# The first chunks of a fused linear-attention and SoLU kernel, written out by hand, with constant matrix products in TensorE's gaps

## The chip, the cores and the metric

The kernel runs on one core of one Trainium2 chip. The time is the device time of one execution in microseconds; the figure compared is the median of several executions. TensorE multiplies matrices out of SBUF into PSUM, VectorE, ScalarE and GpSimd work element by element, and SyncE here only issues DMAs. Each engine takes its instructions in the order in which they were written down, and waits by semaphore for what other engines or DMAs must deliver first.

## What is computed

Two layers follow each other. The first is linear attention with a decay (4 batches, 8 heads, 768 steps, 48 channels a head), the second a feed-forward layer whose activation is SoLU followed by a layer norm:

```python
for t in range(S):
    cur = np.einsum('bhd,bhe->bhde', u[None] * kt, vt)
    y[:, :, t] = np.einsum('bhd,bhde->bhe', rt, state + cur)
    state = w[None, :, :, None] * state + np.einsum('bhd,bhe->bhde', kt, vt)
x = y.transpose(0, 2, 1, 3).reshape(B * S, H * D)        # 3072 x 384
h = x @ w_in                                             # 384 x 1024
solu = h * softmax(h)
out = (layernorm(solu) * g_ln) @ w_out                   # 1024 x 384
```

r, k, v, w and u are float32; w_in, w_out and g_ln are handed over as given by numpy, the weights in float64.

## The kernel before

The sequence is cut into chunks of 128 steps, so there are 24 units (a batch and a chunk each), and `units` lists the first chunk of all four batches, then the second, and so on. Here "chunk 0, 1, 2 ..." means the unit with that index. For each unit:

- `load` fetches r, k and v (192 KB each) into rotating buffers (5 for r and k, 6 for v).
- `decay_k` (L672 to L676, GpSimd) multiplies k by the table `kdec`; `turn_r` and `turn_k` (TensorE) transpose r and k, four 128x128 transposes each; VectorE multiplies the transposed r by the table `fore` (L711), ScalarE copies the transposed k (L720). Chunk 0 takes its undecayed k instead, and VectorE multiplies by `back` (L722).
- `weigh` (two multiplications) and `sum_own` (a row sum on VectorE, L692) give the weight that u adds for a step's own key; `diagonal` writes it as eight 128x128 diagonals (ScalarE, L698) into the tile `AT`.
- `scores` multiplies k by r (TensorE, L733, 16 products, all chunks into the same PSUM tile `at`), then VectorE copies the upper triangle into `AT` with a mask (L735).
- `finish` multiplies v by `AT`, and the state by r from the second chunk of a batch on (TensorE, L760: "heads"), ScalarE copies the result to `xT` (L772), TensorE makes the state's increment (L778), and VectorE and GpSimd update the state (L784 to L787).
- `ffn_in` makes h, the input product: 128 x 384 times 384 x 1024, in two halves of 512 columns (L795), into one PSUM tile `h`, of which there is one buffer; ScalarE takes its exponential (L798).
- `unit` makes the activation and its sums (VectorE L805, L807; ScalarE L809, L810), `halve_ln` and `join_ln` transpose it by DMA, `ffn_out` makes the output product (L877) and stores it.

The weights come in 14 pieces (six of w_in, eight of w_out), as pairs of 32-bit words, and are turned into float32 on the chip: `load_weights` fetches a piece into one of six buffers, `convert_a` makes the low words (ScalarE, L517), `convert_b` the high words (VectorE, L530 and L532), `convert_c` adds them (GpSimd, L540). For the first six pieces `convert_b` uses the PSUM tile `h` as scratch. Pieces 0 to 2 are the three row blocks of w_in's first half of columns, 3 to 5 those of the second.

At the very start w is fetched (L482), transposed (L598) and turned on VectorE into powers and two tables (L599 to L609), whose transposes are `kdec` and `rdec` (L620, L621).

The order of all engines is written out by hand: under `manual_schedule` the instructions stand in each queue in the order of the program text. A loop from i = -2 interleaves the stages of different units; the feed-forward half of a unit lags `LA` = 2 and the output product another `LO` = 5 steps behind. Its first four steps, with a dictionary that says how many pieces each takes up, are the start:

```python
conversions = {-2: 1, -1: 1, 0: 2, 1: 2, 2: 2, 3: 2, 4: 2, 5: 2}
for i in range(-2, N + LA + LO):
    j, l = i - LA, i - LA - LO
```

PSUM tiles of the transposes, heads, state products and output products share the tag `m`, four buffers taken in turn; a buffer's next user waits until its last reader is through.

Of the kernel before, what the change touches and what calls it, by code (L numbers as in the profile page):

```python
# [399 lines left out]
def direct_path(  # L400
# [78 lines left out]
    wrow = const.tile([1, dm], F32, name="wrow")  # L479

    nc.vector.memset(wq, 1.0)
    nc.sync.dma_start(out=wq[:, :, 0:D], in_=w.rearrange("(a q) d -> a q d", q=2))  # L482
    nc.scalar.dma_start(out=u_bc.rearrange("p h d -> p (h d)"),
                        in_=u.rearrange("h d -> (h d)").partition_broadcast(128))
    for i in range(NLD):
# [34 lines left out]
    def convert_b(j):  # L520
        hi, low = step[j]
        n = low.shape[1]
        ma = wpool.tile([128, n], U32, tag="ma", name="ma", bufs=4)
        part = ma
        if pieces[j][2] is None:
            part = psH.tile([128, dff], F32, tag="h", name="part").bitcast(U32)[:, 0:n]

        nc.vector.tensor_scalar(out=part, in0=hi, scalar1=3, scalar2=0x3FFFFFF8,  # L530
                                op0=ALU.logical_shift_left, op1=ALU.bitwise_and)
        nc.vector.scalar_tensor_tensor(out=ma, in0=hi, scalar=0xC0000000, in1=part,  # L532
                                       op0=ALU.bitwise_and, op1=ALU.bitwise_or)
        step[j] = ma, low

    def convert_c(j):
        dst, _, f = pieces[j]
        ma, low = step[j]

        nc.gpsimd.tensor_tensor(out=dst.bitcast(U32) if f is None else ma, in0=ma, in1=low,  # L540
                                op=ALU.add)
# [21 lines left out]
    load(0, "kr")  # L563
    load_weights(0)
    load(1, "kr")
    load_weights(1)
    load(2, "kr")
    load_weights(2)
    load_weights(3)
    load(0, "v")  # L570
    load(3, "kr")
    load_weights(4)
    load(1, "v")
    load_weights(5)
    load(4, "kr")
    load(2, "v")

    ident = const.tile([128, 128], F32, name="ident")
    make_identity(nc, ident)
    for vt in vts:  # L580
        nc.gpsimd.memset(vt[:, :, D:], 0.0)
    neg_half = const.tile([128, 1], F32, name="neg_half")
# [4 lines left out]
    for St in states:  # L587
# [8 lines left out]
    nc.vector.memset(back[:, :, T - 1 : T], 1.0)  # L596
    wd_ps = psM.tile([128, HP], F32, tag="m", name="wd_ps")
    nc.tensor.transpose(wd_ps, wq.rearrange("a q d -> a (q d)"), ident[0:HP, 0:HP])  # L598
    nc.vector.tensor_scalar(out=pw[:, 0, 0], in0=wd_ps, scalar1=LOW, scalar2=HIGH,  # L599
                            op0=ALU.max, op1=ALU.min)  # L600
    for j in range(8):
# [123 lines left out]

    def scores(i):
        X = live[i]
        A4 = X["AT"].rearrange("p (a q) t -> p q a t", q=2)
        for a in range(HP):
            for c in range(2):  # L730
                for q in range(2):
                    rows = slice(q * P, q * P + D)
                    nc.tensor.matmul(pss[ts(c, P), q, a, c * P :], X["kT"][rows, a, ts(c, P)],  # L733
                                     X["rT"][rows, a, c * P :], start=True, stop=True)
        nc.vector.copy_predicated(A4, later.unsqueeze(1).to_broadcast([128, 2, HP, T]), pss)  # L735


# [8 lines left out]
    inner = [[(m,) + p for m in range(g, 12, 4) for p in parts(m)] for g in range(4)]  # L746
    inner = [group[n] for n in range(4) for group in inner]

    def finish(i):
        b, c = units[i]  # L750
        X = live[i]
        vt, AT, St = vts[i % NV], X["AT"], states[b]
        vf = vt.rearrange("p h d -> p (h d)")
        y_ps = psM.tile([128, KD, 128], F32, tag="m", name="y_ps")
        last = {m: n for n, (m, h, at) in enumerate(inner)}
        opened = set()

        def into(m, lhsT, rhs, stop):
            j, g = divmod(m, 4)
            nc.tensor.matmul(y_ps[32 * g : 32 * g + 32, j, :], lhsT, rhs, start=(g not in opened),  # L760
                             stop=stop, skip_group_check=True)
            opened.add(g)

        if c > 0:
            for m in range(12):
                a, n = divmod(m, 3)
                into(m, St[:, a].rearrange("p q d -> p (q d)")[:, ts(n, 32)], X["rT"][:, a, :],
                     False)
        for n, (m, h, at) in enumerate(inner):
            into(m, vf[:, at : at + 32], AT[:, h, :], last[m] == n)  # L770
        X["xT"] = fpool.tile([128, KD, 128], F32, name="xT", bufs=LA + 1)
        nc.scalar.copy(out=X["xT"], in_=y_ps)  # L772
        if c < C - 1:
            kv_ps = psM.tile([128, HP, D], F32, tag="m", name="kv_ps")
            for a in range(HP):
                for g in range(4):
                    h = 2 * a + g // 2
                    nc.tensor.matmul(kv_ps[ts(g, 32), a], X["kp"][:, h, ts(g % 2, 32)],  # L778
                                     vt[:, h, 0:D], start=True, stop=True)
            for q in range(2):  # L780
                wT = pw[ts(q, P), 0, 7].unsqueeze(2).to_broadcast([P, HP, D])
                S = St[ts(q, P), :, q]
                if c > 0:
                    nc.vector.tensor_add(S, kv_ps[ts(q, P)], S)  # L784
                    nc.gpsimd.tensor_mul(S, S, wT)  # L785
                else:
                    nc.vector.tensor_mul(S, kv_ps[ts(q, P)], wT)  # L787


    def ffn_in(i):  # L790
        X = live[i]
        h_ps = psH.tile([128, dff], F32, tag="h", name="h_ps")
        for n in range(dff // NX):
            for j in range(KD):
                nc.tensor.matmul(h_ps[:, ts(n, NX)], X["xT"][:, j, :], w_in_sb[:, j, ts(n, NX)],  # L795
                                 start=(j == 0), stop=(j == KD - 1))
        e = X["e"] = fpool.tile([128, dff], F32, name="e")
        nc.scalar.activation(out=e, in_=h_ps, func=ACT.Exp, accum_out=sums[:, i : i + 1])  # L798
        X["h"] = h_ps

    def unit(i):
        X = live[i]
# [78 lines left out]


    ahead = 6
    todo = list(range(len(pieces)))
    conversions = {-2: 1, -1: 1, 0: 2, 1: 2, 2: 2, 3: 2, 4: 2, 5: 2}
    now = []
    for i in range(-2, N + LA + LO):
        j, l = i - LA, i - LA - LO
        early = l < 0
        if i == -1:  # L890
            nc.sync.dma_start(out=g_sb, in_=moe_g_ln.rearrange("(c p) -> p c", p=128))
        if 0 <= i and i + 5 < N:
            load(i + 5, "kr")
        if 0 <= i and i + 3 < N:
            load(i + 3, "v")
        early_h = l <= 0
        if early_h and i >= LA:
            ffn_in(j)
        before, now = now, [todo.pop(0) for _ in range(conversions.get(i, 0))]
        for p in before:  # L900
            if pieces[p][2] is not None:
                convert_c(p)
        if i == -2:
            turn_r(0)
            turn_k(0)
            turn_table(back, kdec)
            weigh(0, nc.vector)
            decay_k(0)
            sum_own(0)
        for p in now:  # L910
            convert_a(p)
            if ahead < len(pieces):
                load_weights(ahead)
                ahead += 1
        if -2 < i and i + 2 < N:
            if i + 2 < FIRST:
                turn_r(i + 2)
            elif not early_h:
                join_rk(i + 2)
            if early_h and i >= LA:  # L920
                unit(j)
            if early_h and i + 2 >= FIRST:
                join_rk(i + 2)
            if i < 0 or i >= LA:
                sum_own(i + 2)
            if i + 2 < FIRST:
                turn_k(i + 2)
        if i < LA:
            for p in now:
                convert_b(p)  # L930
        if i == 0:
            sum_own(2)
        if i + 3 < N and i != 1:
            decay_k(i + 3)
            if i + 3 >= FIRST:
                decay_r(i + 3)
            if i < 0:
                weigh(i + 3, nc.gpsimd)
        for p in now if i < LA else []:
            convert_c(p)  # L940
        if i == 1:
            weigh(3, nc.gpsimd)
            decay_k(4)
        if 1 <= i and i + 3 < N:
            weigh(i + 3, nc.gpsimd)
        if 0 <= j - 1 < N:
            deviation(j - 1)
# [12 lines left out]
        if not early:  # L960
# [6 lines left out]
            if l == N - 1:  # L967
                check_sums()
            ffn_out(l)
        if 0 <= i + 1 < N:  # L970
            scores(i + 1)
        if i < 0:
            diagonal(i + 2)
        if 0 <= i < N:
            finish(i)
        if i == 1:
            turn_table(fore, rdec)
            sum_own(3)
        if early and 0 <= i:
            diagonal(i + 2)  # L980
        if i == 1:
            nc.vector.tensor_single_scalar(out=minus_g, in_=g_sb, scalar=-1.0, op=ALU.mult)
        if i >= LA:
            for p in before:
                convert_d(p)
            for p in now:
                convert_b(p)
    return bad


# [40 lines left out]
```

## Time and profile before

| | |
|---|---|
| median of 3 runs | 354.89 us (354.72 to 355.54) |
| the profiled execution | 355.35 us, of which the span of the program is 353.5 |
| TensorE busy | 338.0 us, 96% of the span |
| VectorE, ScalarE, GpSimd busy | 210.8, 242.1, 176.5 us |
| first instruction of TensorE | at 3.59 us |
| first input product starts | at 27.63 us |
| second input product starts | at 36.77 us |
| loads up to the sixth weight piece | landed at 24.04 us |

In lines of the profile, PE is TensorE, DVE is VectorE, ACT is ScalarE, POOL is GpSimd, SP is SyncE, and L733 is line 733 of the kernel. In lists by time the first column is the start in us after the span's begin and the second the length of that group; instructions of one kind that follow each other are merged, with their number behind an x (a float32 product is two instructions there, and a transpose one), and the square brackets tell how long the engine was idle before and what ended that. In the chain that ended last each line is a stretch of the one chain of dependent work, traced back from the end. In the list of waits the three figures are the sum in us, the number of times, and the longest.

### The profile page before, as it was taken

How to read it: one execution, taken by the hardware profiler on the slowest of the kernel's cores; microseconds unless marked ns; L12 is line 12 of the kernel's file. 1: busy time of each engine (PE TensorE's matmuls, PEld its weight loads, DVE VectorE, ACT ScalarE, POOL GpSimd, SP SyncE). 2: the span in 40 equal slices, each digit the busy share in tenths (PEclk: the TensorE clock that was granted, in tenths of full speed). 3: DMA queues.
4: the chain of work that ended last, by engine and by line, in shares of the span. 5: the costliest groups of instructions: out<-in, count | busy, mean ns of one | idle time of the engine just before them, and what ended most of it. 6: DMA issues, size and time to landing. Idle time of an engine off the chain costs nothing.

```text
span 353.5 us, 8407 instructions
## 1 busy us (share of the span) xinstructions
PE 338.0 (96%) x3427; PEld 204.8 (58%) x3427; DVE 210.8 (60%) x323; ACT 242.1 (68%) x457; POOL 176.5 (50%) x196
## 2 busy tenths in 40 slices
PE   2699999999999999999999999999999999999993
PEld 2485566656566556566566566565565565555563
DVE  7795888886468567665865765765771441323220
ACT  3765988988897667677867778778687464465510
POOL 3879667784865754945945846746730000000000
PEclk9999999999999999999999999999999999999998
DMA  7998997259999868988997979857663523551641
GB/s 164 266 237 183 252 209 126 51 105 162 189 186 163 150 122 154 195 174 185 188 159 174 206 146 184 187 130 146 150 129 62 126 69 59 128 126 47 139 105 33
DMA packets 164878, 52.75 MB, mean 149 GB/s; under 512 B 157917, under 2 KB 161246, under 8 KB 164830
## 3 DMA queue, kind: packets, MB, share of 16 engines
q1 hardware_dynamic: 164686, 51.92, 71.9%
q8 instruction: 29, 0.48, 0.6%
q10 hardware_dynamic: 144, 0.20, 0.2%
q14 instruction: 19, 0.16, 0.2%
HBM read 26.94 MB, written 4.72 MB: 90 GB/s over the span
## 4 chain that ended last, share of the span: by engine, by line
PE 90%; issue 3%; POOL 2%; DVE 2%; ACT 1%; DMA 1%; POOLq 0%; DVEq 0%
PE o_ps L877 35%; PE h_ps L795 35%; PE y_ps L760 10%; PE at L733 6%; PE kv_ps L778 2%; PE tk_ps L718 1%; PE tr_ps L710 1%; POOL kp L674 1%; DMA wq<-in_w_dram 1%; ACT AT L698 1%; POOL rku L687 1%; DVE part L530 0%; DVE ma L532 0%; POOL w_in_sb L540 0%; DVE solu L807 0%
## 5 line engine op out<-in xcount | busy, mean ns | idle before, releaser
L795 PE MATMUL h_ps<-w_in_sb,xT 128*128 128x512 f32 x288 | 129.8, 600 | 0.7 <-DVE solu L807 0.5
L877 PE MATMUL o_ps<-w_out_sb,lnT 128*128 128x384 f32 (+1 forms) x400 | 127.3, 473 | 0.0
L877 PEld LDWEIGHTS o_ps<-w_out_sb,lnT 128*128 128x128 f32 x400 | 75.1, 190 | 52.8 <-issue 9.1
L795 PEld LDWEIGHTS h_ps<-w_in_sb,xT 128*128 128x128 f32 x288 | 52.8, 190 | 60.7 <-issue 58.1
L698 ACT ACTIVATE AT<-ident,own 128x128 f32<-128x128 f32 x192 | 58.6, 391 | 6.2 <-DVE own L692 6.2
L785 POOL TENSOR_TENSOR state<-state,pw 64x192 f32<-64x192 f32 x32 | 25.6, 800 | 63.2 <-DVE state L784 62.0
L735 DVE COPY_PREDICATED AT<-later,at 128x1024 f32<-128x1024 uint32 x24 | 31.9, 1329 | 31.4 <-PE at L733 31.4
L845 ACT COPY halves<-solu 128x2048 uint16<-128x2048 uint16 x24 | 45.4, 1893 | 0.0
L839 DVE COPY lnT<-halves 128x2048 uint16<-128x2048 uint16 x24 | 37.4, 1559 | 11.7 <-DMA halves<-halves 11.7
L809 ACT ACTIVATE solu<-solu,st 128x1024 f32<-128x1024 f32 x24 | 27.5, 1148 | 22.6 <-DVE solu L807 22.6
L798 ACT ACTIVATE e<-h_ps 128x1024 f32<-128x1024 f32 x24 | 24.5, 1021 | 18.3 <-PE h_ps L795 18.3
L816 POOL TENSOR_SCALAR st<-st 128x1 f32<-128x1 f32 x24 | 7.0, 292 | 59.2 <-ACT e L810 59.2
L674 POOL TENSOR_TENSOR kp<-kpad,kdec 128x512 f32<-128x512 f32 x24 | 31.6, 1317 | 7.6 <-ACT kdec L621 6.5
L807 DVE SCALAR_TENSOR_TENSOR solu<-h_ps,st,e 128x1024 f32<-128x1024 f32 x24 | 30.8, 1284 | 2.5 <-DVE st L805 0.5
L688 POOL TENSOR_TENSOR rku<-rku,rpad 128x384 f32<-128x384 f32 x23 | 28.9, 1256 | 1.8
L839 DVE COPY rk<-halves 128x2048 uint16<-128x2048 uint16 x15 | 21.7, 1444 | 11.4 <-DMA halves<-halves 11.0
L733 PE MATMUL at<-rk 48*64 48x128 f32 (+1 forms) x768 | 27.9, 265 | 0.0
L733 PEld LDWEIGHTS at<-rk 48*64 48x64 f32 x768 | 21.8, 139 | 10.4 <-issue 8.8
L681 POOL TENSOR_TENSOR rp<-rpad,rdec 128x512 f32<-128x512 f32 x15 | 27.4, 1829 | 0.0
L860 DVE COPY halves<-rp 128x1024 uint16<-128x1024 uint16 x15 | 19.8, 1319 | 11.3 <-POOL rp L681 11.3
L760 PE MATMUL y_ps<-AT,vt 128*32 128x128 f32 x768 | 26.3, 279 | 0.0
L810 ACT ACTIVATE e<-solu 128x1024 f32<-128x1024 f32 x24 | 25.4, 1057 | 0.8
(82 smaller groups left out, 320.3 us busy)
## 6 DMA issues: line engine op xcount, KB each, us to landing
raw<-in_moe_w_in_dram SPq DMA_DIRECT2D x12, 512.0 KB, 5.7
raw<-in_moe_w_out_dram SPq DMA_DIRECT2D x16, 384.0 KB, 4.7
kpad<-in_k_dram SPq DMA_DIRECT2D x24, 192.0 KB, 4.2
rpad<-in_r_dram SPq DMA_DIRECT2D x24, 192.0 KB, 4.6
vt<-in_v_dram SPq DMA_DIRECT2D x24, 192.0 KB, 4.5
out_dram<-o SPq DMA_DIRECT2D x23, 192.0 KB, 2.2
halves<-halves SPq DMA_TRANSPOSE x39, 4.6
u_bc<-in_u_dram ACTq DMA_DIRECT2D x1, 192.0 KB, 3.8
```

What stands on the lines that cost most here:

```text
L674: nc.gpsimd.tensor_mul(X["kp"].rearrange("p h d -> p (h d)"), kpads[i % NLD].rearrange("p h d -> p (h d)"), kdec.rearrange("p a d -> p (a ...
L688: engine.tensor_mul(rku, rku, rpads[i % NLD][:, :, 0:D])
L698: nc.scalar.activation(out=AT[:, h, :], in_=ident, func=ACT.Copy, scale=X["own"][:, h])
L733: nc.tensor.matmul(pss[ts(c, P), q, a, c * P :], X["kT"][rows, a, ts(c, P)], X["rT"][rows, a, c * P :], start=True, stop=True)
L735: nc.vector.copy_predicated(A4, later.unsqueeze(1).to_broadcast([128, 2, HP, T]), pss)
L760: nc.tensor.matmul(y_ps[32 * g : 32 * g + 32, j, :], lhsT, rhs, start=(g not in opened), stop=stop, skip_group_check=True)
L795: nc.tensor.matmul(h_ps[:, ts(n, NX)], X["xT"][:, j, :], w_in_sb[:, j, ts(n, NX)], start=(j == 0), stop=(j == KD - 1))
L807: nc.vector.scalar_tensor_tensor(out=solu, in0=X["h"], scalar=rs, in1=X["e"], op0=ALU.mult, op1=ALU.mult, accum_out=tot)
L809: nc.scalar.activation(out=solu, in_=solu, func=ACT.Identity, scale=-float(dff), bias=tot)
L839: nc.vector.tensor_copy(out=words.bitcast(U16).rearrange("p n (t o) -> p o n t", o=2), in_=turned)
L845: nc.scalar.copy(out=both.rearrange("p (o n) -> p o n", o=2), in_=split(X["solu"]))
L877: nc.tensor.matmul(o_ps, X["lnT"][:, f, :], w_out_sb[:, f, part], start=(f == 0), stop=(f == KF - 1))
```

## The change

The start is no longer made by the loop: the calls for the first chunks are written out one by one, and the loop begins at i = 2. On the way some functions are cut so that their parts can stand apart in the queues: `scores` loses its masked copy to `take_scores`, `finish` becomes `heads`, `take_y` and `update`, and `ffn_in` can make one half of the columns at a time.

- `spin(n)` issues n plain 128x128 products of the identity with itself into the tile `h`; nothing reads them. There are six such calls, 21 products.
- The load of w moves from SyncE's DMA queue to ScalarE's, ahead of u. The loads of v for chunks 0 and 1 and the last weight pieces move up in SyncE's queue, and so does g.
- `weigh(0)` moves from VectorE to GpSimd.
- The scratch of `convert_b` for the first six pieces moves from the tile `h` to the shared tag `m`.
- The first input product is made in two halves, with the conversions of pieces 3 to 5 beside the first. In TensorE's queue the scores of chunk 2 stood ahead of it and still do, and the heads of chunk 2 behind it; the transposes of chunk 3 and of the table for `rdec`, which stood ahead, move behind the heads of chunk 2.
- At i = 2 the loop issues the rest of what it issued there before, and from i = 3 on the same as before.

```diff
-    nc.sync.dma_start(out=wq[:, :, 0:D], in_=w.rearrange("(a q) d -> a q d", q=2))
+    nc.scalar.dma_start(out=wq[:, :, 0:D], in_=w.rearrange("(a q) d -> a q d", q=2))
...
-            part = psH.tile([128, dff], F32, tag="h", name="part").bitcast(U32)[:, 0:n]
+            part = psM.tile([128, n], F32, tag="m", name="part").bitcast(U32)
...
     load(0, "kr")
     load_weights(0)
     load(1, "kr")
+    load(0, "v")
     load_weights(1)
     load(2, "kr")
     load_weights(2)
+    load(1, "v")
     load_weights(3)
-    load(0, "v")
+    load_weights(4)
+    load_weights(5)
     load(3, "kr")
-    load_weights(4)
-    load(1, "v")
-    load_weights(5)
+    load(2, "v")
     load(4, "kr")
-    load(2, "v")
+    nc.sync.dma_start(out=g_sb, in_=moe_g_ln.rearrange("(c p) -> p c", p=128))
 
     ident = const.tile([128, 128], F32, name="ident")
     make_identity(nc, ident)
+
+    def spin(n):
+
+        ps = psH.tile([128, dff], F32, tag="h", name="spin")
+        for _ in range(n):
+            nc.tensor.matmul(ps[:, 0:128], ident, ident, start=True, stop=True)
+
+    spin(3)
...
     nc.tensor.transpose(wd_ps, wq.rearrange("a q d -> a (q d)"), ident[0:HP, 0:HP])
+    spin(5)
...
+    def take_scores(i):
+        A4 = live[i]["AT"].rearrange("p (a q) t -> p q a t", q=2)
         nc.vector.copy_predicated(A4, later.unsqueeze(1).to_broadcast([128, 2, HP, T]), pss)
...
-    def ffn_in(i):
+    def ffn_in(i, halves=(0, 1)):
         X = live[i]
-        h_ps = psH.tile([128, dff], F32, tag="h", name="h_ps")
-        for n in range(dff // NX):
+        if 0 in halves:
+            X["h"] = psH.tile([128, dff], F32, tag="h", name="h_ps")
+        h_ps = X["h"]
+        for n in halves:
             for j in range(KD):
                 nc.tensor.matmul(h_ps[:, ts(n, NX)], X["xT"][:, j, :], w_in_sb[:, j, ts(n, NX)],
                                  start=(j == 0), stop=(j == KD - 1))
+        if 1 not in halves:
+            return
...
+    def take_up(p):
+        nonlocal ahead
+        convert_a(p)
+        if ahead < len(pieces):
+            load_weights(ahead)
+            ahead += 1
+
+    turn_r(0)
+    turn_k(0)
+    turn_table(back, kdec)
+    weigh(0, nc.gpsimd)
+    decay_k(0)
+    sum_own(0)
+    diagonal(0)
+    take_up(0)
+    spin(2)
+    scores(0)
+    convert_b(0)
+    decay_k(1)
+    weigh(1, nc.gpsimd)
+    turn_r(1)
+    spin(4)
+    turn_k(1)
+    take_scores(0)
+    convert_c(0)
+    sum_own(1)
+    take_up(1)
+    diagonal(1)
+    spin(3)
+    heads(0)
+    convert_b(1)
+    convert_c(1)
+    scores(1)
+    update(0)
+    take_y(0)
+    decay_k(2)
+    turn_r(2)
+    take_up(2)
+    spin(4)
+    turn_k(2)
+    take_scores(1)
+    convert_b(2)
+    convert_c(2)
+    weigh(2, nc.gpsimd)
+    load(5, "kr")
+    load(3, "v")
+    heads(1)
+    scores(2)
+    take_up(3)
+    take_y(1)
+    convert_b(3)
+    convert_c(3)
+    sum_own(2)
+    ffn_in(0, (0,))
+    take_up(4)
+    convert_b(4)
+    convert_c(4)
+    load(6, "kr")
+    load(4, "v")
+    take_up(5)
+    diagonal(2)
+    convert_b(5)
+    convert_c(5)
+    ffn_in(0, (1,))
+    take_scores(2)
+    update(1)
+    decay_k(3)
+    heads(2)
+    turn_r(3)
+    take_y(2)
+    turn_k(3)
+    decay_k(4)
+    weigh(3, nc.gpsimd)
+    turn_table(fore, rdec)
+    update(2)
+    sum_own(3)
+    diagonal(3)
+    weigh(4, nc.gpsimd)
...
+    todo = list(range(6, len(pieces)))
     now = []
-    for i in range(-2, N + LA + LO):
+    for i in range(LA, N + LA + LO):
...
-        if early_h and i >= LA:
+        if early_h and i > LA:
             ffn_in(j)
```

## The prediction

> **What bounds the kernel now.** I read the page's share of busy time first, then TensorE's instructions in order of time, then the chain that ended last, then the list of waits.
>
> ```profile
> span 353.5 us, 8407 instructions
> PE 338.0 (96%) x3427; PEld 204.8 (58%) x3427; DVE 210.8 (60%) x323; ACT 242.1 (68%) x457; POOL 176.5 (50%) x196
> ```
>
> TensorE is idle for 15.5 us in all. Next, its instructions by start, length and idle time before:
>
> ```profile
> 3.59 0.23 PE L598 MATMUL wd_ps<-ident,wq 4*128 4x4 f32 x1 [3.59 <-DMA wq<-in_w_dram]
> 6.78 1.08 PE L710 MATMUL tr_ps<-ident,rpad 128*128 128x128 f32 x4 [2.95 <-DMA rpad<-in_r_dram]
> ...
> 10.43 1.12 PE L710 MATMUL tr_ps<-ident,rpad 128*128 128x128 f32 x4 [0.86 <-DMA rpad<-in_r_dram]
> 12.92 1.11 PE L718 MATMUL tk_ps<-ident,kp 128*128 128x128 f32 x4 [1.37 <-POOL kp L674]
> 13.96 1.97 PE L733 MATMUL at<-rk 48*64 48x128 f32 x32
> ...
> 17.43 1.12 PE L718 MATMUL tk_ps<-ident,kp 128*128 128x128 f32 x4 [0.45 <-POOL kp L674]
> 18.47 1.97 PE L733 MATMUL at<-rk 48*64 48x128 f32 x32
> 20.38 1.94 PE L760 MATMUL y_ps<-AT,vt 128*32 128x128 f32 x32
> ...
> 24.42 1.09 PE L733 MATMUL at<-rk 48*64 48x128 f32 x32
> 25.44 1.08 PE L760 MATMUL y_ps<-AT,vt 128*32 128x128 f32 x32
> ...
> 27.63 5.42 PE L795 MATMUL h_ps<-w_in_sb,xT 128*128 128x512 f32 x12 [0.18 <-DVE ma L532]
> ...
> 36.77 5.39 PE L795 MATMUL h_ps<-w_in_sb,xT 128*128 128x512 f32 x12 [0.48 <-DVE solu L807]
> ```
>
> Two things are to be seen. Nearly all the idle time is at the front: after 36.77, where the second chunk's input product starts, the chain is TensorE back to back. And the same 32 score products take 1.97 us up to 20.4 and 1.09 from 24.4. Single transposes shorten from 421 to 273 ns between 23.7 and 24.3, so the array runs at half speed until about 24.0 (the row of granted clocks says full speed there: it does not record this).
>
> The chain shows who leads before the first input product: GpSimd and VectorE as much as TensorE.
>
> ```profile
> 11.60 1.27 POOL kp L674
> ...
> 25.36 0.70 DVE ma L532
> ...
> 33.42 0.68 ACT AT L698 x2
> ```
>
> ```profile
> POOL kp L674 <- ACT kdec L621: 6.5, 1, 6.5
> ```
>
> So GpSimd stands until 10.28 for the decay table. What the change is worth is therefore one number: when the second input product (call it H1) starts, 36.77 now, plus whatever the queues behind it then lose. From there both orders give TensorE the same work.
>
> **The change, part by part.** I walk each queue in its new order: an instruction starts when its engine is free and its last input is there, plus 0.03 us. Start-to-start prices, from the rows: four transposes 0.445 us at full speed, scores 1.02, heads 0.88, state products 0.46, half an input product 2.65, all times 1.93 at half speed (0.85 a transpose group, 1.91 scores); VectorE: scaled copy of a transpose 0.60 (0.69 to its result), conversion 0.72 then 0.69, row sum 0.47 (0.55), masked copy 1.21 (1.32), state 0.72, activation product 0.18 and 1.30; ScalarE: copy 0.48 (0.58), eight diagonals 2.36 (2.45), low words 0.59; GpSimd: decay 1.23 (1.27), weights 1.24 (1.28), weighing 1.09 and 0.97. The same walk through the old order, with its landing times, puts H1 at 36.44 and the third product H2 at 44.99; the profile has 36.77 and 45.33. I compare walk with walk.
>
> *Loads.* w leaves SP's queue, where it was issued from 1.06 to 1.92; ScalarE could issue at 0.79. So k and r of chunk 0 start about 1.1 us earlier: r lands at 5.6 instead of 6.64. Everything behind follows in the new order at the old spacings (about 0.9 us for a k, r or v, 1.75 for a weight piece): the sixth piece at 21.9 instead of 24.04, v of chunk 2 at 24.7 instead of 27.6. u now waits behind w on ScalarE's queue: 4.59 becomes 5.8. Its reader is the weighing, which moves to GpSimd: 5.83 to 7.92, ahead of the row sum at 8.38. The four state clears end at 5.5 instead of 4.24; ScalarE's next work comes after 7.7. Both are covered; VectorE is rid of two weighing steps of 0.55 us. Loads of g and of the next chunks move behind a further weight piece; they have 4 us of slack in the walk (5 us late costs 0.55).
>
> *Constant products.* 21 of them in six groups. One is two passes over 128 columns; a pass over 512 took 5.39/12 = 0.45 us, so one costs 0.22, or 0.43 at half speed: 4.7 to 9.0 us in all, in program order. At half speed the first three (1.38 to 2.67) are free while w is awaited; the five behind the w transpose run 3.76 to 5.90, while r lands at 5.6: 0.3 us on the path. From there TensorE has no gap until 16.0 at half speed. Groups two, four, three and four come before the products that read k or the masked copy. At full speed those still wait after them (0.3 to 1.0 us in each place), so they are free; at half speed they are on the path.
>
> When does full speed come? In the rows, a stretch without a gap from 12.92 to 16.98 (4.1 us: transposes and scores) did not bring it; the one from 17.43 had brought it by 24.0 (6.55 us; 3.6 us after heads 0 began at 20.38). The new stretch starts at 3.76: full speed at 7.8 to 10.3.
>
> *The Trainium skill, "TensorE: Matmul & The Clock Gate", Part 1, says that the clock opens after one busy window of some 3.4 us, and that the window runs freely; that would be 7.2 to 10.6 from 3.76, an estimate, or earlier if the first three count: a sum of -1.0 to -1.75. Its Part 4 says that transposes do not count as busy in the same way, which speaks against the cover from 5.9 to 8.5. No view here tells the two apart.*
>
> *Chunks 0 and 1, warm at 7.8.* Tables done at 7.15, kdec at 8.8 (was 10.2), decays to 11.4, weighing of chunk 1 to 13.46, its row sum, conversion of piece 1 to 15.4 on VectorE, that piece on GpSimd to 16.7, decay of chunk 2 to 17.97, transpose at 18.0, heads 1 18.45, scores 2, first half of H0 at 20.8 (H0 was 27.63 in the profile).
>
> Scores, heads and state update are cut into parts without an instruction more; what moves is the turn of VectorE and ScalarE, as walked here: chunk 1's scaled r copy now goes ahead of chunk 0's masked copy (which waits for its diagonals till 11.6 anyway).
>
> *H0 in halves.* The first half needs pieces 0 to 2, there by 20.6. The second waits on GpSimd and VectorE: piece 2 ends 20.6, weighing 2 22.65, row sum 23.2, conversions of pieces 4 and 5 to 26.0, GpSimd's last piece 27.3. Pieces 3, 4 and 5 open gaps of about 0.5, 1.1 and 0.5 us, and H0 ends at 28.2 instead of 32.9. So the stall on pieces goes from 0.18 to 2 us, but 7 us earlier.
>
> *Behind H0.* Heads 2, once between H0 and H1, plus transposes 3 and 4, table and scores 3. The conversions' scratch now turns in the four shared PSUM buffers, so heads 2 waits for state 1, and the r transpose of chunk 4 for state 2 (idle 0.6). The chain from there: r transpose 31.97, row sum and scaled copy 32.9, sums, activation 33.1 to 34.4, H1 at 34.44 after another 1.0 us idle for the old H0 buffer. Against 36.44: -2.0.
>
> *Given back.* The diagonals of chunk 3 used to run before the exponential; now they wait for a row sum at 32.3 and end near 34.8, so ScalarE still has them, two low words, two activations, a copy and chunk 4's diagonals when H1 ends. H1's exponential starts 1.0 us late, and H2 waits 0.54 where it waited 0. Sum: 43.53 - 44.99 = -1.45 at H2, and it stays so at H3 and H4. Warm at 10.3 gives -1.0. Both ends are kept; I take -1.3. The profiled execution lasted 355.35 us (1.85 around its span) and would become 354.05; the median of the three is 0.46 below it, so 353.6.
>
> **Rivals.** *A, slower: the clock opens late.* The stretch that failed was transposes and 48x64 score products; if these do not count, the 2.1 us of constant products up to 5.90 may be too few, and the next dense stretch is constant products and heads 0 from 14.7 to 17.4. Every microsecond of delay past 10.3 then costs 0.5: opening at 13.0 is break-even, 17.0 gives H1 at 37.85 and +1.95 (356.8). For it: that stretch, and that 5.90 to 16.0 is again mostly transposes and scores. Against: 20 full 128x128 passes before 5.90.
> *B, the early front is worth nothing:* VectorE and GpSimd hold H1. w lands after k and r have started, and all of the chain hangs on it: each 0.1 us of w is 0.1 us in the end. 1 us late: -0.75 if warm early, -0.3 to 0 if warm at 10. Sixth piece 3 us later than my spacing: 0 too. For it: 2 us of gaps in H0.
> *C, better:* warm before 6.5, if 3.6 us count from the three first products on (1.38 + 3.6 = 5.0): -1.75 (353.1), where the tables bind and no earlier opening helps.
>
> **How the numbers follow.** Forecast case 0.45 (-0.8 to -1.6), C 0.17 (-1.6 to -2.4), B 0.16 (-0.7 to +0.5), A 0.22 (+0.5 to +2.4). Bounds of the walk add 0.4 either way. Range 352.4 to 356.2 leaves out half of A's upper part and C's far end; the likeliest case alone is 353.0 to 354.4. 0.2% (0.7 us) is about what a measurement tells from none: faster by that is the forecast and C, less a little of the forecast's edge, 0.60; within it most of B and a rim of A, 0.17; slower 0.23.
>
> **What would show it.** Right: transposes or scores near 0.45 and 1.0 us by about 10; kdec about 1.4 us earlier; H0's first half near 21 with gaps before its last three pairs; H1 near 34.8; a short wait at H2 for VectorE's activation product. Wrong: scores at 1.9 us still at 14; H1 after 36; TensorE waiting for a load after 20; a fall back to half speed in H0's gaps.

## The result, and the profile after

The changed kernel takes 355.21 us (355.02 to 355.89, 4 runs), the kernel before in the same comparison 354.82 us (354.72 to 355.54, 4 runs): a ratio of 1.001, with a 95% interval from 0.9991 to 1.0029. A second comparison on another chip, with twelve runs of the new kernel against 23 of the old, gave 1.0007 (0.9997 to 1.0018). So the change makes no difference that can be measured. The forecast was 353.6, faster by 1.3 us.

The profiled execution lasted 355.02 us with a span of 353.3, where before it was 355.35 and 353.5. First the page's head and its share of busy time:

```profile
span 353.3 us, 8488 instructions
PE 339.7 (96%) x3469; PEld 206.4 (58%) x3469; DVE 210.4 (60%) x321; ACT 242.3 (69%) x457; POOL 178.7 (51%) x198
```

TensorE has 42 instructions more (21 products of two passes each) and is idle for 13.6 us instead of 15.5. The constant products are busy for 7.7 us (the six groups' 1.65, 2.50, 0.61, 1.06, 0.83 and 1.06), yet the busy time rose by 1.7 only: some 6.0 us of other work fell away, which fits the products that ran at half speed up to 24.0 before. Then TensorE's instructions by start, length and idle time before:

```profile
3.99 0.23 PE L607 MATMUL wd_ps<-ident,wq 4*128 4x4 f32 x1 [0.93 <-DMA wq<-in_w_dram]
4.15 2.50 PE L586 MATMUL spin<-ident 128*128 128x128 f32 x10
7.13 1.09 PE L720 MATMUL tr_ps<-ident,rpad 128*128 128x128 f32 x4 [0.48 <-DMA rpad<-in_r_dram]
8.01 0.66 PE L728 MATMUL tk_ps<-ident,kpad 128*128 128x128 f32 x4
...
9.60 1.09 PE L742 MATMUL at<-rk 48*64 48x128 f32 x32
...
14.59 1.08 PE L772 MATMUL y_ps<-AT,vt 128*32 128x128 f32 x32 [0.64 <-DVE AT L747]
...
22.21 2.84 PE L819 MATMUL h_ps<-w_in_sb,xT 128*128 128x512 f32 x6
25.64 1.12 PE L819 MATMUL h_ps<-w_in_sb,xT 128*128 128x512 f32 x2 [0.59 <-POOL w_in_sb L540]
27.75 1.12 PE L819 MATMUL h_ps<-w_in_sb,xT 128*128 128x512 f32 x2 [0.98 <-POOL w_in_sb L540]
29.07 1.13 PE L819 MATMUL h_ps<-w_in_sb,xT 128*128 128x512 f32 x2 [0.20 <-POOL w_in_sb L540]
...
36.28 5.42 PE L819 MATMUL h_ps<-w_in_sb,xT 128*128 128x512 f32 x12 [1.25 <-DVE solu L832]
...
45.20 5.39 PE L819 MATMUL h_ps<-w_in_sb,xT 128*128 128x512 f32 x12 [0.26 <-DVE solu L832]
```

Three things are to be seen. The clock is early: the first score products, at 9.60, already take 1.09 us, where they took 1.97 up to 20.4 before. The first input product starts at 22.21, which is 5.4 us earlier than before, but has 1.8 us of gaps before its last three pairs. And the second, H1, starts at 36.28, only 0.49 us earlier; the third, H2, at 45.20, 0.13 us earlier. That is the whole effect, and it agrees with spans that differ by 0.2 us.

The chain that ended last, over the first 38 us, says who leads now (start, length, what):

```profile
2.36 5.53 DMA u_bc<-in_u_dram
...
8.03 1.00 POOL rku L697
...
9.12 1.01 POOL rku L698
...
10.15 0.56 DVE own L702
...
10.74 2.46 ACT AT L708 x8
...
13.22 1.33 DVE AT L747
...
22.27 1.01 POOL rku L697
...
23.36 1.00 POOL rku L698
...
24.39 0.55 DVE own L702
```

Before, the chain came from the powers of w over the tables to GpSimd's decay. Now it comes from the load of u: GpSimd cannot weigh chunk 0 until u is there, and the row sum, the eight diagonals, the masked copy and heads 0 at 14.59 stand in line behind that. The list of waits answers to the 6.5 us that GpSimd stood for `kdec` before:

```profile
POOL rku L697 <- DMA u_bc<-in_u_dram: 4.2, 1, 4.2
```

The page's list of DMA issues (size, and microseconds from issue to landing) has the load itself; issued at 2.36, behind the 1.26 us that ScalarE's queue spent on issuing w, it took 5.5 us and landed at 7.89. Before, it was issued at 0.79, took 3.8 and landed at 4.59.

```profile
u_bc<-in_u_dram ACTq DMA_DIRECT2D x1, 192.0 KB, 5.5
```

VectorE's row of the later part of the same chain, by start, length and idle time:

```profile
24.39 0.55 DVE L702 TENSOR_REDUCE own<-rku 128x8 f32<-128x384 f32 x1 [2.16 <-POOL rku L698]
```

VectorE stands 2.16 us for GpSimd's weighing of chunk 2, and the conversions of the fourth to sixth weight pieces stand behind the row sum: this makes the gaps in the first input product. The change itself brought that order about: in the kernel before, GpSimd weighed chunk 2 at 17.33, directly behind its decay at 16.10, and piece 1 came after it; in the new order the weighing stands behind piece 2. The list of the change's parts does not name this move.

### The profile page after: what moved, and what is told of

The parts are those of the page before. It is cut to its first block, busy times and chain, and to the rows that moved or that the text cites. A ratio compares the mean times of both kernels' runs of the same rounds, so it can differ in the third digit from the quotient of the medians.

```text
span 353.3 us, 8488 instructions
## 1 busy us (share of the span) xinstructions
PE 339.7 (96%) x3469; PEld 206.4 (58%) x3469; DVE 210.4 (60%) x321; ACT 242.3 (69%) x457; POOL 178.7 (51%) x198
## 4 chain that ended last, share of the span: by engine, by line
PE 86%; ACT 3%; POOL 3%; DVE 3%; DMA 2%; issue 1%; ACTq 0%; POOLq 0%
PE o_ps L902 35%; PE h_ps L819 33%; PE y_ps L772 10%; PE at L742 6%; ACT AT L708 2%; PE kv_ps L789 2%; DMA u_bc<-in_u_dram 2%; POOL rku L698 1%; POOL rku L697 1%; DVE AT L747 1%; POOL kp L684 1%; PE tr_ps L720 1%; DVE own L702 0%; DVE ma L532 0%; PE tk_ps L728 0%
## 5 line engine op out<-in xcount | busy, mean ns | idle before, releaser
L698 POOL TENSOR_TENSOR rku<-rku,rpad 128x384 f32<-128x384 f32 x24 | 29.9, 1244 | 1.9
L697 POOL TENSOR_TENSOR rku<-kpad,u_bc 128x384 f32<-128x384 f32 x24 | 26.3, 1095 | 4.2 <-DMA u_bc<-in_u_dram 4.2
L742 PE MATMUL at<-rk 48*64 48x64 f32 (+1 forms) x768 | 26.2, 255 | 0.0
L742 PEld LDWEIGHTS at<-rk 48*64 48x64 f32 x768 | 20.4, 132 | 9.9 <-issue 7.9
L772 PE MATMUL y_ps<-AT,vt 128*32 128x128 f32 x768 | 25.5, 273 | 0.6 <-DVE AT L747 0.6
```

The costliest lines, as they stand in the source:

```text
L697: engine.tensor_mul(rku, kpads[i % NLD][:, :, 0:D], u_bc)
L698: engine.tensor_mul(rku, rku, rpads[i % NLD][:, :, 0:D])
```

## The experiments

Two theories came from these rows. The first: u, late on ScalarE's queue, costs the forecast's gain; bring it early again and it comes back. The second: the order of GpSimd's queue around chunk 2 costs it. A third question was what the constant products are worth alone. All edits are against the changed kernel unless said otherwise, and every ratio is against the kernel before on the same chip.

### u ahead of w, the weighing of chunk 2 earlier, and both

First, u ahead of w in ScalarE's queue:

```diff
-    nc.scalar.dma_start(out=wq[:, :, 0:D], ...)
     nc.scalar.dma_start(out=u_bc..., in_=u...)
+    nc.scalar.dma_start(out=wq[:, :, 0:D], ...)
```

> The changed kernel with one edit: on ScalarE's DMA queue u is issued first and w behind it. Theory 1 (the late u ate the gain): u lands near 4.6 instead of 8.0, w some 0.4 us later than now, chunk 0's weighing on GpSimd starts before 7 instead of at 8.03, its row sum near 9.3 instead of 10.15; H1 starts near 35.4 instead of 36.28, and the time is 0.8 us below the changed kernel, 0.5 to 0.9 below the kernel before. Rival (the conversions and the weighing of chunk 2 hold H1 whatever chunk 0 does): H1 within 0.2 us of 36.28 and no change. A second rival: w now late, H1 36.3 or later.

356.82 us (356.63 to 357.12), ratio 1.0058 (1.0045 to 1.0071): slower by 2 us, as the second rival had it. u landed at 4.81, but w, 1.5 KB, now waited behind it. TensorE's row:

```profile
5.70 0.24 PE L607 MATMUL wd_ps<-ident,wq 4*128 4x4 f32 x1 [2.64 <-DMA wq<-in_w_dram]
```

The transpose of w came 1.71 us later than in the changed kernel, the tables were done 3.0 us later (10.4 against 7.4), and the end was 1.6 us later. The other 1.3 us of the tables' delay is in two rows of VectorE:

```profile
6.17 0.66 DVE L613 TENSOR_TENSOR pw<-pw 128x4 f32<-128x4 f32 x1
...
6.95 0.97 DVE L616 COPY tab<-pw 128x4 f32<-128x4 f32 x1
```

In the changed kernel these two steps take 0.16 and 0.17 us. Here GpSimd weighed chunk 0 beside them, from 5.82 to 6.81 and from 6.89 to 7.90, and each of the two ended just after one of its multiplications. Whether an early u is worth anything this run can't say.

Second, the weighing of chunk 2 taken ahead of the conversions in GpSimd's queue:

```diff
     decay_k(2)
+    weigh(2, nc.gpsimd)
     turn_r(2)
...
     convert_c(2)
-    weigh(2, nc.gpsimd)
```

> The changed kernel with one edit: the two weighing multiplications of chunk 2 move on GpSimd from behind weight piece 2 to directly behind chunk 2's decay; u still late. GpSimd stood idle from 19.2 to 21.0 there, waiting for piece 2's high words, and VectorE then stood 2.16 us waiting for that weighing with the conversions of pieces 4 and 5 behind it. Theory 1 (both u and this order hold H1, one after the other): the wait of 2.16 us goes, the second half of H0 ends near 28 instead of 30.1, H1 starts near 34.2 and the time is 2.0 us below the changed kernel, some 1.9 below the kernel before. Rival (only u counts): within 0.3 us of the changed kernel.

352.35 us (352.09 to 352.50), ratio 0.9932 (0.9919 to 0.9945). This version beats both kernels: 2.5 us less than the one before. VectorE's row sum of chunk 2 stands without a wait, and TensorE has the first input product in one piece:

```profile
21.55 0.54 DVE L702 TENSOR_REDUCE own<-rku 128x8 f32<-128x384 f32 x1
```

```profile
21.62 5.73 PE L819 MATMUL h_ps<-w_in_sb,xT 128*128 128x512 f32 x12
...
33.45 5.42 PE L819 MATMUL h_ps<-w_in_sb,xT 128*128 128x512 f32 x12 [1.27 <-DVE solu L832]
42.37 5.39 PE L819 MATMUL h_ps<-w_in_sb,xT 128*128 128x512 f32 x12 [0.25 <-DVE solu L832]
```

H1 is 2.83 us ahead of the changed kernel's. Of this 0.59 was there at the first input product already (21.62 against 22.21: in this execution u landed at 7.30 and was read at 7.44 instead of 8.03; heads 0 is earlier by the same 0.59), so the move itself is worth 2.24 at H1. GpSimd used to stand from 19.2 to 21.0 for VectorE's high words of piece 2; the 2.1 us of weighing now lie in that idle time instead of behind it.

Third, both edits together:

> Both edits, u first and chunk 2's weighing early. Theory 1: the gains add nearly, H1 near 33.5, 2.9 us below the changed kernel and 2.5 to 2.9 below the kernel before. Rival (one of the two hides the other): no better than the better of the two alone.

354.81 us (354.22 to 355.50), ratio 0.9995 (0.9987 to 1.0004): near the sum of the two as measured, 2.0 us better than u first alone, 2.5 worse than the weighing alone. The 2.5 to 2.9 us that theory 1 expected did not come, since u first alone loses.

### The constant products: none, the first eight, and in the old order

All six calls taken out, in the new order:

```diff
-    spin(3)
-    spin(5)
...
-    spin(2)
-    spin(4)
-    spin(3)
-    spin(4)
```

> The changed kernel without its 21 constant products; nothing else differs, and the output does not depend on them. Theory 1 (they bring full speed at 8.1 instead of about 18 to 24): scores of chunks 0 and 1 take 1.9 us each, H1 starts at 38 to 39 and the time is 1.9 to 2.8 us above the changed kernel. Rival (VectorE and GpSimd lead the start in any case, the clock is beside the path): within 0.4 us of the changed kernel.

356.78 us, ratio 1.0038 (1.0016 to 1.006), with a wide spread of executions from 354.48 to 358.63: four of the twelve lie at 354.5 to 354.8, as short as the shorter ones of the changed kernel (354.36 to 356.40 in twelve). By the ratios the products are worth 1.1 us on the mean, less than theory 1 expected and more than its rival. The profiled one, by stretches of 2 us (stretch, its length, busy time of PE, PEld, DVE, ACT and POOL, and then the granted clock, the share of the DMA engines and GB/s):

```profile
12.00:14.00 2.00, 1.04 (x8) 0.65 (x12) 1.31 (x1) 1.97 (x5) 1.92 (x3) 0.58 1.24 238
14.00:16.00 2.00, 2.00 (x52) 1.87 (x56) 1.82 (x3) 1.55 (x6) 1.35 (x2) 0.50 0.99 267
16.00:18.00 2.00, 2.00 (x57) 1.87 (x48) 0.73 (x3) 2.00 (x7) 1.84 (x2) 0.50 0.99 290
18.00:20.00 2.00, 1.80 (x12) 1.25 (x8) 0.60 (x1) 0.27 (x2) 0.66 (x1) 0.71 1.02 396
```

```profile
6.08 1.09 PE L718 MATMUL tr_ps<-ident,rpad 128*128 128x128 f32 x4 [1.91 <-DVE pw L612]
6.96 1.06 PE L726 MATMUL tk_ps<-ident,kpad 128*128 128x128 f32 x4
7.81 1.06 PE L628 MATMUL kd_ps<-ident,tab 128*128 128x128 f32 x4
8.80 1.13 PE L740 MATMUL at<-rk 48*64 48x128 f32 x32
...
13.91 1.94 PE L770 MATMUL y_ps<-AT,vt 128*32 128x128 f32 x32 [0.83 <-DVE AT L745]
```

The clock opened here too, at 8.93 by the trace's record of it (the scores at 8.80 take 1.13 us). But it fell back to half at 12.3 and came back at 19.2: a mean of 0.58 over 12 to 14 is full speed for 0.32 us, one of 0.71 over 18 to 20 is half speed for 1.16. Heads 0 and scores 1 ran at half speed; chunk 0's scores had full speed, against the expectation.

Only the first two calls kept, 8 products of the 21:

```diff
     spin(3)
     spin(5)
...
-    spin(2)
-    spin(4)
-    spin(3)
-    spin(4)
```

> The changed kernel with only the first two groups of constant products (three and five); the later four groups, 13 products, left out. Without any, the clock record showed full speed from 8.9 to 12.3, half speed to 19.2, then full speed. Theory 1 (the first eight open the clock, the later 13 keep it open while TensorE waits for GpSimd): full speed from 7 to 11, then in most executions a fall to half speed for one or two periods of 3.41 us, scores or heads of chunks 0 or 1 at 1.9 us, and a time 0.5 to 2.5 us above the changed kernel, with more spread. Rival (once open it stays open through waits of 1 to 2 us, and the 13 do nothing): within 0.3 us of the changed kernel, as narrow.

357.30 us (356.08 to 357.71), ratio 1.0055 (1.0035 to 1.0076), where all of them gave 1.0007: 1.7 us more. The clock was full from 7.03, and in 12.19 to 12.85 the k transposes still took 0.66. TensorE stood 1.49 us before them and 1.31 behind them, and at 13.85 the clock fell to half, till 17.27:

```profile
14.15 1.93 PE L772 MATMUL y_ps<-AT,vt 128*32 128x128 f32 x32 [1.31 <-DVE AT L747]
```

So the thirteen keep the clock open over the gaps of this start. What the first eight add is not shown: without any the clock opened too, at 8.93, and the intervals of the two versions, 1.0016 to 1.006 and 1.0035 to 1.0076, overlap.

Last, the kernel before, with only `spin(3)` and `spin(5)` put in at the same places:

```diff
+    spin(3)
     for vt in vts:
...
     nc.tensor.transpose(wd_ps, wq..., ident[0:HP, 0:HP])
+    spin(5)
```

> The kernel before with the first two groups of constant products alone (three once the identity is there, five behind the transpose of w). Theory 1 (in the old order GpSimd's decays lead the start): full speed opens by 7 to 12 and may fall back; scores of chunk 0 may take 1.0 us, but H1 moves by 0.2 to 0.9 us at most, and the time is 0 to 0.9 us below the kernel before. Rival (the cold array is what the old start lost): H1 2 us earlier or more.

355.32 us (354.94 to 356.20), ratio 1.001 (0.9997 to 1.0023). The clock opened at 8.30 and fell back at 11.72 till 21.96. In the old order opening it for 3.4 us buys nothing that can be measured; H1 came at 36.43 in its profile, 0.34 earlier. What holding it would buy there was not tried.

### w back on SyncE's queue, u alone on ScalarE's

This leaves everything else new, and makes both w and u early:

```diff
-    nc.scalar.dma_start(out=wq[:, :, 0:D], ...)
+    nc.sync.dma_start(out=wq[:, :, 0:D], ...)
```

> The changed kernel with w back at the head of SP's queue, u alone on ScalarE's, as before the change; all else new. The run with u first had w behind u's 192 KB in the same queue: its transpose started at 5.70 instead of 3.99, and the tables with it. Theory 1 (either small load behind the other on ScalarE's queue costs what it is late): u lands near 4.6, the w transpose starts near 3.6, r of chunk 0 lands at 6.6 to 6.7 as in both kernels, chunk 0's weighing starts near 5.8, H1 starts near 35.4 and the time is 0.9 us below the changed kernel, 0.5 to 0.9 below the kernel before. Rival (k and r of chunk 0, issued 1.1 us later, cost what w and u bring): no change against the changed kernel.

355.33 us (354.85 to 356.47), ratio 1.0008 (0.9995 to 1.002). My first theory falls here: w's transpose started at 3.89, u landed at 3.84, 4.0 us earlier than in the changed kernel, r at 6.39, and nothing came of it. GpSimd's and VectorE's rows of this kernel show a loss in its place:

```profile
5.47 1.00 POOL L697 TENSOR_TENSOR rku<-kpad,u_bc 128x384 f32<-128x384 f32 x1 [1.67 <-DMA kpad<-in_k_dram]
6.55 0.99 POOL L698 TENSOR_TENSOR rku<-rku,rpad 128x384 f32<-128x384 f32 x1
```

```profile
5.55 1.00 DVE L619 TENSOR_TENSOR tab<-tab,pw 128x64 f32<-128x64 f32 x1
...
6.64 1.06 DVE L619 TENSOR_TENSOR tab<-tab,pw 128x128 f32<-128x128 f32 x1
...
7.78 1.11 DVE L619 TENSOR_TENSOR tab<-tab,pw 128x256 f32<-128x256 f32 x2
```

In the changed kernel, where GpSimd still stood for u, the same two steps took 0.19 and 0.25 us:

```profile
5.66 0.19 DVE L619 TENSOR_TENSOR tab<-tab,pw 128x64 f32<-128x64 f32 x1
...
5.93 0.25 DVE L619 TENSOR_TENSOR tab<-tab,pw 128x128 f32<-128x128 f32 x1
```

A small VectorE product that begins while GpSimd multiplies ends just after GpSimd does: 6.55 after 6.47, 7.70 after 7.54. Twice 0.8 us is lost on the tables, which were done at 8.9 instead of 7.4, and all chains go through the tables: chunk 0's row sum, the first step behind its weighing, began at 10.21, where it began at 10.15 in the changed kernel. In this execution the clock opened late as well, at 13.04, so that the first scores took 1.97 us; it lasted 356.31 us, 1.0 above the median, and its H1 at 37.22 is therefore not the collision's alone.

The Trainium skill, "SBUF — State Buffer", section "SBUF: two separate sides", has this rule: VectorE and GpSimd share one pair of ports as an exclusive lock, and a VectorE operation with two SBUF inputs and a GpSimd operation that reads SBUF shut each other out for a whole instruction. The rows agree, with 0.19 us becoming 1.00.

Then w back and the weighing of chunk 2 early (the second edit above) together:

> w back on SP's queue and chunk 2's weighing early. Theory 1: H1 at 33.2 to 33.6, 2.7 to 3.4 us below the kernel before, that is 0.4 to 0.9 below the run with the weighing alone (352.35). Rival (TensorE's work and the waits behind H0 now hold H1): the same as the weighing alone.

352.95 us (352.61 to 353.52), ratio 0.9939 (0.9921 to 0.9956). The weighing is worth 2.4 us here too; bringing u earlier adds nothing to it, as the rival had it. Two VectorE products of only 4 elements a lane took 0.96 us each there. The clock opened at 7.74, as early as in the run with the weighing alone (7.61), and chunk 0's row sum began at 10.15 again.

### w back, and the weighing of chunk 0 back on VectorE

If the collision is the cause, it goes when GpSimd does not weigh beside the tables:

```diff
-    nc.scalar.dma_start(out=wq[:, :, 0:D], ...)
+    nc.sync.dma_start(out=wq[:, :, 0:D], ...)
...
-    weigh(0, nc.gpsimd)
+    weigh(0, nc.vector)
```

> The changed kernel with w back at the head of SP's queue (as in the run before) and chunk 0's weighing back on VectorE, behind its scaled copy of k. In the run with w back alone, the two weighing multiplications ran on GpSimd from 5.47 to 7.54, and in that time VectorE's table products of 64 and 128 columns took 1.00 and 1.06 us, each ending as a GpSimd instruction ended, where the same two take 0.19 and 0.25 in the changed kernel. Theory 1 (a VectorE product with both inputs in SBUF waits out a GpSimd instruction that runs beside it): the two take 0.2 and 0.25 again, the tables end near 7.4 instead of 8.9, the row sum comes near 10.1, and H1 starts near 36.0 to 36.4: about 1 us below the run with w back alone, the same as the changed kernel within 0.4 us. Rival (the table products were slowed by the loads landing then): 1 us again, H1 at 37 or later.

355.72 us (354.99 to 356.27), ratio 1.0019 (1.0009 to 1.0029). The tables were fast again, which the collision demands: 0.19 and 0.26 us for the same two steps, done by 7.2. But the time did not follow; H1 came at 37.29 where 36.0 to 36.4 was expected. VectorE's and GpSimd's rows:

```profile
5.51 0.19 DVE L619 TENSOR_TENSOR tab<-tab,pw 128x64 f32<-128x64 f32 x1
...
9.46 1.59 DVE L698 TENSOR_TENSOR rku<-rku,rpad 128x384 f32<-128x384 f32 x1
```

```profile
9.38 2.82 POOL L684 TENSOR_TENSOR kp<-kpad,kdec 128x512 f32<-128x512 f32 x2 [5.57 <-ACT kdec L631]
```

The collision moved: VectorE's second weighing step began just as `kdec` let GpSimd's decay go, and took 1.59 us instead of the 0.56 that it took before, and the two decays 2.82 instead of 2.50. Chunk 0's row sum began at 11.09 instead of 10.15, its diagonals at 11.68 instead of 10.74, heads 0 at 15.59 instead of 14.59. So the collision on the tables is shown to come and go with GpSimd's weighing; that the time would be better without any collision is not shown by this run. With the weighing of chunk 2 early as well:

> The same with chunk 2's weighing moved up on GpSimd as well. Theory 1: H1 at 33.6 to 34.0, 2.0 us below the kernel before, no better than the weighing alone with the loads as changed (352.35). Rival (u and w early are worth something once nothing collides): 0.5 us or more below 352.35.

353.69 us (353.03 to 353.82), ratio 0.9958 (0.9945 to 0.9971): 2.0 us better than without, but about 1 behind the best version. In the profiled execution of this one the step at L698 took 0.56 us from 9.69: `kdec` was copied at 9.36 instead of 8.71, GpSimd's decay began at 10.03, when that step was already under way, and VectorE did not wait. Yet the row sum began at 10.29, since VectorE now did the weighing itself behind its two scaled copies. So in no version with u early did chunk 0's row sum come before 10.15.

### The changed kernel again

> The changed kernel itself once more, on the chip of the last two, for a closer interval. Both views: within 0.3% of the kernel before, H1 near 36.3 if the clock opens by 10, with some executions up to 1 us longer where it opens later.

355.08 us (354.36 to 356.40, 12 runs), ratio 1.0007 (0.9997 to 1.0018). H1 was at 36.36 in its profiled execution, against 36.28 in the first, although the clock opened at 9.94 instead of 8.13, and r of chunk 0 landed at 6.15 instead of 7.00. What did not differ is u, which landed at 7.95 and 7.89. VectorE's row sum of chunk 0 stood for it:

```profile
10.21 0.55 DVE L702 TENSOR_REDUCE own<-rku 128x8 f32<-128x384 f32 x1 [1.13 <-POOL rku L698]
```

## Why the prediction was right or wrong

The forecast gain of 1.3 us did not come. The stated range, 352.4 to 356.2, holds the result of 355.21, but by its width, which takes in rival B and part of A; the likeliest case alone, 353.0 to 354.4, does not hold it.

**What bounds it: right.** The gain was read as the start of H1 plus what the queues behind it lose. H1 came 0.49 earlier than before, 0.36 of it was given back by H2, and the span is 0.2 shorter.

**The clock: right.** Full speed was forecast for 7.8 to 10.3, and came at 8.13 and 9.94. Rival A's loss, with the clock late at 17, did not come. Taking out the constant products, or thirteen of them, costs 1.1 and 1.7 us (ratios of 1.0038 and 1.0055 against 1.0007), so within the new order a clock that stays open is worth about that much. An opening at 10.3 instead of 7.8 was priced at 0.45 us; the two profiles of the changed kernel, 1.8 us apart in the opening, differ by 0.08 at H1. At this start VectorE and GpSimd lead, not TensorE.

**Loads: the step that failed.** It said that r of chunk 0 lands at 5.6 instead of 6.64, that u goes from 4.59 to 5.8, and that this is covered. r landed at 7.00 (6.15 in the second profile), u at 7.89, and GpSimd's weighing started at 8.03 instead of 5.83. The spacing of the old order was carried over to a queue in which everything is earlier and denser: the first k did land at 3.80 instead of 5.76, but u was issued 1.57 us later than before, with three loads of the other queue ahead of it, and took 5.5 us instead of 3.8. From there each later step is 1.2 to 2.2 us behind its forecast:

| step | forecast | measured |
|---|---|---|
| weighing of chunk 0 done | 7.92 | 10.12 |
| weighing of chunk 1 done | 13.46 | 14.62 |
| piece 1 added on GpSimd | 16.7 | 17.96 |
| heads 1 | 18.45 | 19.84 |
| first half of the first input product | 20.8 | 22.21 |
| end of the first input product | 28.2 | 30.2 |
| H1 | 34.44 | 36.28 |

(The walk puts the old H1 0.33 us before the profile's, so its 34.44 stands for 34.8 in a profile.) Of the two loads it is u that held the start: between the two profiles of the changed kernel r's landing differs by 0.85 us, u's by 0.06 and H1 by 0.08, and in the run with the weighing moved u was read 0.59 us earlier and heads 0 and the first input product came 0.59 earlier. What u costs is bounded by the row sum of chunk 0, which stood 0.60 us for the weighing in the first profile and 1.13 in the second: at most 1.1 us of the 1.5 that H1 is late. The rest was not taken apart.

**"Rid of two weighing steps": a second error, hidden by the first.** The weighing on GpSimd was costed at its own length beside VectorE's tables. Had u landed at 5.8 as forecast, the collision seen with w back would have fallen on the last table steps; that is inferred, since in no run did u land then. The late u kept GpSimd out of the way, which was luck. At the start the trace of before could not show the collision, for GpSimd did nothing there between 3.8 and 10.28. But it has others, where GpSimd is the one that waits. Its weighing usually takes 1.00 us; beside a long VectorE copy it took twice that:

```profile
105.14 1.34 DVE L839 COPY rk<-halves 128x2048 uint16<-128x2048 uint16 x1 [3.18 <-DMA halves<-halves]
```

```profile
105.26 2.05 POOL L687 TENSOR_TENSOR rku<-kpad,u_bc 128x384 f32<-128x384 f32 x1
```

I should have bounded it from both sides, as a step whose neighbour is new, and did not.

**The first input product: right in kind.** Gaps of 0.5, 1.1 and 0.5 us were forecast and 0.59, 0.98 and 0.20 measured; 1.0 us of waiting for the old buffer at H1, and 1.25 measured. The wait at H2 was 0.26, not 0.54. The rows for this stood in the prediction ("the second waits on GpSimd and VectorE: piece 2 ends 20.6, weighing 2 22.65"), but it took the order as given and did not say that this line is the dearest of the start: moved in one queue, back to where the old order had it, it gives 2.2 us.

**The rivals.** B named the outcome (the early front is worth nothing because VectorE and GpSimd hold H1) and a wrong culprit: it hung on w, which was 0.4 us later, while u was 3.3 us later. Its chance of 0.16 was too small, since the same step held all landing times of a reordered queue.

What stays open: why r of chunk 0 lands hardly earlier or later than before (6.15 and 7.00 against 6.64) with k ahead by 2.0 us was not taken apart, and neither was the clock's spread between kernels. No run shows the gain that an early u would bring without a collision. A version in which GpSimd's weighing of chunk 0 waits until the tables are done, with u early, was not tried.

## What to carry to other kernels

A load's landing in a reordered queue is not its old landing moved by the time its issue moved; bound it by the latest as well, and ask what the first reader of the last-issued load holds up. When work moves to an idle engine, look at what its neighbour does in that time: "covered" was true of the engine and false of what it shares. And read a long wait in the new order as an offer: the 2.16 us of VectorE behind GpSimd's weighing needed one line moved, and made the kernel 0.7% faster, where the change as it stood made nothing.

## What the runs showed of the hardware

- A VectorE product of two SBUF operands beside a GpSimd multiplication waits for the end of the GpSimd instruction: 0.19 us became 1.00, 0.25 became 1.06, and 0.56 became 1.59. A product of 4 elements a lane (0.15 us) took 0.96, and a copy of 4 elements a lane (0.17) took 0.97. The other way round, a GpSimd multiplication of 1.00 us took 2.05 beside a VectorE copy that had begun first. VectorE's products with one operand in PSUM were not touched: the scaled copy at 8.26, beside GpSimd's weighing from 8.03, took its usual 0.69.
- A load of 1.5 KB behind one of 192 KB in the same queue was there 1.7 us later than ahead of it (5.70 against 3.99, by the start of its reader). The 192 KB behind the 1.5 KB took 5.5 us instead of 3.8 to land; they were also issued 1.57 us later, with three loads of the other queue ahead, so which of the two made them slow is not shown. Issuing the 1.5 KB took ScalarE's queue 1.26 us, issuing the 192 KB 0.36.
- The clock's changes after its first opening are 3.4 us or a multiple of it apart: 12.3 to 19.2 (two), 13.85 to 17.27 (one, with the first eight products), 11.72 to 21.96 (three, in the old order). This agrees with the free-running period of some 3.4 us that the Trainium skill gives in "TensorE: Matmul & The Clock Gate", Part 1. It also states that the clock falls after an idle period; here the one that ended at 12.3 held 1.54 us of idle time in 3.41, so a partly idle one was enough. In the changed kernel, where the thirteen products stand, the one from 11.55 to 14.96 held 1.03 us of idle time (0.39 and 0.64), and the clock stayed full.
- Whether transposes count is not settled. Without constant products the clock opened at 8.93, and the 3.41 us before that held nothing but twelve transposes (6.08 to 8.8) and the first 0.13 us of scores. Part 4 of that page says that they do not count in the same way; this run does not bear that out. But with w back the 3.41 us from 6.22 to 9.63 held about as much, the same twelve transposes but for the last few and 0.3 us of constant products, and the clock opened one period later, at 13.04. And before the change 4 us of transposes and scores from 12.92 on did not open it; how much the 48-row score products count was not measured.
- The opening varied from 7.03 to 13.04 us between kernels whose first constant products stand at nearly the same times, and by 1.8 us between two executions of one kernel.
